# A new order for the attention units, a shorter first slot table, and list positions cast by threes

## The chip, the core and the metric

The kernel runs on one core of a Trainium2 chip. TensorE is written PE here (its weight loads PEld), VectorE DVE, ScalarE ACT, GpSimd POOL and SyncE SP; each runs its own instructions in the order in which they were issued, and waits on semaphores for the others. The metric is the device time of one execution in microseconds (us).

## The reference

Packed attention, and behind it a mixture of experts with one expert per row. There are 8 batches of 8 heads, 576 positions and 64 elements per head; p has 32 packed queries per head.

```python
def sm_attn(qq, kk, vv):                       # softmax(qq kk^T / 8) vv
    ...
p_packed = sm_attn(p, k, v)                    # 32 rows per head
out = sm_attn(q, p_packed, p_packed)           # 576 rows per head
x = out.transpose(0, 2, 1, 3).reshape(4608, 512)

logits = x @ w_gate + modality_bias[modality_id]     # [4608, 8]
e_idx = np.argmax(logits, axis=1)
gate_w = softmax(logits)[arange, e_idx]
for e in range(8):                                    # F = 1024
    out[mask_e] = gate_w[mask_e] * (np.maximum(x[mask_e] @ w1[e], 0) @ w2[e])
```

## The kernel before, in words

**Attention** is cut into 8 units: a unit is one pair of batches and one half of the heads. A unit consists of named steps, each a generator's next stretch:

- `dk`, `dq`, `dv`: loads of k, q and v, issued by SP. k and q go to the tiles rek and req, of which there are two each.
- `k0`-`k4`, `q0`-`q4`: PE turns k and q (L231), ACT copies the result out of PSUM to kT (L234).
- `c0`, `c1`: scores of the packed queries (L246 on PE), the maximum on DVE (nb, L257), exp on ACT (L261). `r`: reciprocals of the sums on DVE (L267 to L269).
- `a0`-`a2`: PE turns these weights (L275), ACT copies them (L278). `p`, given three times or more: weights times v on PE (L289, called the pack below), DVE scales and masks them (bd, L297; pd, L301).
- `t`: PE turns pd (L308), ACT copies it (ppT, L312). `g`: the gate's product (L322, L325).
- `s0`, `s1`, each given several times: scores of all queries against the packed keys (L246 on PE), then on DVE a transposing read (st, L333), maximum (L336), subtraction (L338), sum (L343), reciprocal (L347), product (L349) and a transposition back (a2T, L355); exp is ACT's (L340).
- `x0`-`x2`: the output of the unit and its gate logits (L371 on PE), copied by ACT (xs, L382), the logits by DVE (lt, L384). `w`: SP writes xs to DRAM as x_scr (L396, L397).

PSUM has four buffers for transpositions (ps1) and two for scores, packs and outputs (ps2), so a step that needs a buffer waits for the reader of the one before it.

**The order** of all this on PE, DVE, ACT and SP is written out by hand: the string `ORDER` is run once for every n from -6 on, and `>` or `<` in front of a name takes the step of unit n+1 or n-1 instead of n. `e` runs a piece of other work (the preparation of p, L169 to L174, and the routing of rows that are complete), `f` a piece of `scatter`, which writes row numbers to lists in DRAM by POOL: a list position is cast to an integer on DVE (L485) and used by one indirect DMA (L486). Units 0 to 6 run in this loop wholly; of unit 7 only `d k c q a r p` do.

**Behind the loop** comes the mixture. Rows of one expert fill slots of two tiles of 128 rows. A slot table (`table_phase`) says which expert and which list rows each slot has; there are three, a, b and c, each made from the rows that are routed by then. Table a is computed on DVE near the end of the loop. The first expert's w1 is loaded early, or loaded again if table a names another one (the `If` at L867, which waits in SP's queue behind what stands there). ACT rounds w1 to its high part (w1h, L672), DVE takes the rest (w1l, L673), rows are fetched by POOL (L677, L679), turned by PE (L692), and multiplied: L712 is the first product (h), L747 the second. The rest of unit 7 (`t g s0 s1 x0 x1 x2 w`) runs within slot 0.

Of the kernel before, what the change touches and what calls it, by code (L numbers as in the profile page):

```python
# [8 lines left out]
F32 = mybir.dt.float32  # L9
F32R = mybir.dt.float32r  # L10
BF16 = mybir.dt.bfloat16
I32 = mybir.dt.int32
AF = mybir.ActivationFunctionType
ALU = mybir.AluOpType
# [9 lines left out]
def packed_attn_moe_kernel(  # L24
# [14 lines left out]
    nc = tc.nc  # L39
# [3 lines left out]
    E, _, F = w1.shape  # L43
    P = 128
# [146 lines left out]
    def attention(i, g, lt, A, Z):  # L191
# [217 lines left out]
        for nm, f, args in (("k", trans, [("k", *z) for z in fw]), ("q", trans, [("q", *z) for z in fw]),  # L409
# [3 lines left out]
            for n, z in enumerate(args or [()]):  # L413
# [1 line left out]
        return steps  # L415


    ORDER = ("<f >>c0 e >>>k4 >t >>>k2 s0 >q4 >t >>>k4 >>>k3 e >>dv >q0 >>>k0 >>c0 s0 e >q0 f s0 >>>k2 >>r s0 >s1 >s0 "
# [3 lines left out]

    def run_all(u, order):
        for z in order.split():
# [56 lines left out]

    def scatter(i):
        for c in range(NC):
            dsi = sm.tile([P, 1], I32, name=f"dsi{c}", bufs=2)
            nc.vector.tensor_copy(out=dsi, in_=dests[i][:, c:c + 1])  # L485
            ins = ins_of(nc.gpsimd.indirect_dma_start(  # L486
                out=lst, out_offset=bass.IndirectOffsetOnAxis(ap=dsi, axis=0),
                in_=meta[:, i * NC + c, :], in_offset=None))
            tc.declare_no_dep(ins, group="scat", reason="every row of the list is written once")
            tc.add_to_no_dep_group("scat", ins)  # L490
            if i >= NA[0]:
                tc.add_to_no_dep_group("late", ins)
            if i >= NA[1]:
                tc.add_to_no_dep_group("last", ins)
            scattered[i].append(ins)
            yield ins
# [4 lines left out]
    def st_(nm, w=E, dt=F32):  # L501
        return sm.tile([P, w], dt, name=nm, bufs=2)
# [91 lines left out]
    def table_phase(nm, e_first, n, used, n_slots):  # L594
# [10 lines left out]
        def row_e(starts):  # L605
            r = st_("row_e")
            tsc(out=r, in0=starts, scalar1=sidx, scalar2=-float(P2), op0=ALU.subtract, op1=ALU.mult)
            if used is not None:
# [7 lines left out]
        starts, ends, sel = table(rotated(e_first), tl, row_e, tb)  # L616
        z = slice(0, 1)
        tt(out=tb[z, 3:4], in0=tb[z, 1:2], in1=e_first[z], op=ALU.not_equal)

        pr = st_("pref", 1)  # L620
        tt(out=pr[z], in0=tb[z, 1:2], in1=tb[z, 2:3], op=ALU.subtract)
        nc.vector.scalar_tensor_tensor(out=pr[z], in0=pr[z], scalar=tb[z, 3:4], in1=tb[z, 2:3],
                                       op0=ALU.mult, op1=ALU.add)
        pre_i = const.tile([P, 1], I32, name="pre_" + nm)
        nc.vector.tensor_copy(out=pre_i[z], in_=pr[z])
        used2 = le = None
        if n_slots:
            used2 = const.tile([P, E], F32, name="used_" + nm)
            tsc(out=used2, in0=starts, scalar1=-1.0, scalar2=float(n_slots), op0=ALU.mult, op1=ALU.add)
            tt(out=used2, in0=used2, in1=tl, op=ALU.min)  # L630
            tsc(out=used2, in0=used2, scalar1=0.0, scalar2=None, op0=ALU.max)
            if used is not None:
                tt(out=used2, in0=used2, in1=used, op=ALU.add)
            le = const.tile([P, 1], F32, name="last_" + nm)
            expert_at(starts, ends, float(n_slots - 1), le)
        else:

            one = st_("one")
            nc.vector.scalar_tensor_tensor(out=one, in0=tl, scalar=-float(P2), in1=rem, op0=ALU.mult, op1=ALU.add)
            tsc(out=one, in0=one, scalar1=-float(P), scalar2=None, op0=ALU.is_le)  # L640
            tt(out=one, in0=one, in1=sel, op=ALU.mult)
            tsc(out=ends, in0=ends, scalar1=-1.0, scalar2=sidx, op0=ALU.add, op1=ALU.is_equal)
            tt(out=tb[:, 6:7], in0=dot_e(one, ends), in1=tb[:, 4:5], op=ALU.subtract)
            tsc(out=tb[:, 6:7], in0=tb[:, 6:7], scalar1=-1.0, scalar2=None, op0=ALU.mult)
        return dict(tab=to_int(tb, "tab_" + nm), pre=pre_i, used=used2, last=le)

    def val(tb, s, col, engines, lo, hi):
        return nc.values_load(tb[s:s + 1, col:col + 1], engines=engines, min_val=lo, max_val=hi,  # L648
# [263 lines left out]
    with ExitStack() as actx:  # L912
# [3 lines left out]
        ZL["st"] = (lp, zq)  # L916
        u = us[NU + 1]

        def table_b():
            for _ in routing(NA[1] - 1, lts[NA[1] - 1], ZL["ps1"]):  # L920
                pass
            T.append(table_phase("b", T[0]["last"], NA[1], T[0]["used"], SA[1] - SA[0]))
            todo.append(scatter(NA[1] - 1))

        def behind_both(ins):
            es = ExitStack()
            for z in ins:
# [14 lines left out]
        for n in range(1, 4):  # L942
            ev = st_1(W, todo[0], 3, (2 * n,))
            if n == 1:
                with behind_both(ev):
                    split_w(W, 1, None, (0, 1))
                T.append(table_phase("b", T[0]["last"], NA[1], T[0]["used"], SA[1] - SA[0]))
                tab = next(z for z in reversed(nc.cur_bb.bb.instructions) if z.engine == ET.DVE)
            if n == 2:
                with behind_both(ev):  # L950
                    split_w(W, 1, None, (2, 3))
# [5 lines left out]
        run_all(u, "s1 x0 x1 x2 w")  # L957
        for _ in routing(NA[1], lts[NA[1]], ZL["ps1"]):
            pass
    T.append(table_phase("c", T[1]["last"], NP, T[1]["used"], None))  # L960
    todo.append(scatter(NA[1]))

# [52 lines left out]
```

## Time and profile before

| | before |
|---|---|
| median of 3 runs | 609.91 us (609.74 to 610.02) |
| the profiled execution's own time | 610.75 us |
| its span, first to last instruction | 609.2 us |
| mean granted TensorE clock | 0.984 |
| instructions | 12555 |
| PE busy in the span | 570.3 us (94%) |
| DVE, ACT, POOL busy in the span | 251.7, 220.3, 147.4 us |

The profile is of one execution: its own time lies 1.55 us above its span and 0.84 us above the median of the runs. A busy share over the whole span mixes two stages, the attention (to about 140 us) and the mixture, which have different limits.

### The profile page before, as it was taken

How to read it: one execution, taken by the hardware profiler on the slowest of the kernel's cores; microseconds unless marked ns; L12 is line 12 of the kernel's file. 1: busy time of each engine (PE TensorE's matmuls, PEld its weight loads, DVE VectorE, ACT ScalarE, POOL GpSimd, SP SyncE). 2: the span in 40 equal slices, each digit the busy share in tenths (PEclk: the TensorE clock that was granted, in tenths of full speed). 3: DMA queues.
4: the chain of work that ended last, by engine and by line, in shares of the span. 5: the costliest groups of instructions: out<-in, count | busy, mean ns of one | idle time of the engine just before them, and what ended most of it. 6: DMA issues, size and time to landing. Idle time of an engine off the chain costs nothing. (4 is left out here: it accounts for less than half of the span.)

```text
span 609.2 us, 12555 instructions
## 1 busy us (share of the span) xinstructions
PE 570.3 (94%) x4820; PEld 495.7 (81%) x4820; DVE 251.7 (41%) x657; ACT 220.3 (36%) x401; POOL 147.4 (24%) x183
## 2 busy tenths in 40 slices
PE   4989899879999999999999999999999999999982
PEld 3667576567888988988979988988989989989982
DVE  1588989986956212162112182202112112112281
ACT  3667677664422212172112271212212122112361
POOL 2200041340751422322132122212212211211221
PEclk9989999997999999999999999999999999999998
DMA  9998799858668110139521146101101111111112
GB/s 309 327 332 245 245 374 358 253 158 281 236 233 249 57 53 20 37 108 387 198 68 57 36 134 248 57 36 53 54 36 36 61 46 37 54 35 54 42 49 59
DMA packets 45458, 86.97 MB, mean 143 GB/s; under 512 B 8632, under 2 KB 18552, under 8 KB 45368
## 3 DMA queue, kind: packets, MB, share of 16 engines
q1 hardware_dynamic: 35784, 63.53, 31.1%
q0 software_dynamic: 8528, 22.16, 11.6%
q8 instruction: 49, 0.80, 0.5%
q14 instruction: 41, 0.34, 0.2%
q10 hardware_dynamic: 1056, 0.15, 0.1%
HBM read 66.25 MB, written 19.56 MB: 141 GB/s over the span
## 5 line engine op out<-in xcount | busy, mean ns | idle before, releaser
L712 PE MATMUL ps_h<-x_hl,w1h 128*128 128x256 f32 x1088 | 199.0, 285 | 0.8 <-ACTq L909 0.8
L712 PEld LDWEIGHTS ps_h<-x_hl,w1h 128*128 128x128 f32 x1088 | 171.6, 192 | 4.3 <-ACT x_hl L694 1.0
L712 PE MATMUL ps_h<-x_hl,w1l 128*128 128x256 f32 x544 | 154.4, 284 | 0.0
L717 DVE SCALAR_TENSOR_TENSOR hl<-ps_h,hh 128x512 fp32r<-128x512 f32 x68 | 46.9, 690 | 245.9 <-ACT hh L716 245.8
L747 PE MATMUL ps_o<-w2h,hh 128*128 128x512 f32 x296 | 117.9, 398 | 3.3 <-ACT ot L751 2.2
L747 PE MATMUL ps_o<-w2h,hl 128*128 128x512 f32 x296 | 116.4, 393 | 0.0
L747 PE MATMUL ps_o<-w2l,hh 128*128 128x512 f32 x296 | 115.8, 391 | 0.3 <-DVEq L862 0.3
L712 PEld LDWEIGHTS ps_h<-x_hl,w1l 128*128 128x128 f32 x544 | 104.6, 192 | 0.0
L716 ACT ACTIVATE hh<-ps_h 128x512 fp32r<-128x512 f32 x68 | 40.6, 598 | 151.6 <-PE ps_h L712 150.1
L752 POOL DMA_INDIRECT out_dram<-ot,mt x37 | 40.5, 1094 | 181.4 <-ACT ot L751 112.6
L751 ACT ACTIVATE ot<-ps_o,mt 128x512 f32<-128x512 f32 x37 | 25.4, 687 | 149.7 <-PE ps_o L747 117.7
L747 PEld LDWEIGHTS ps_o<-w2h,hh 128*128 128x128 f32 x296 | 55.7, 188 | 14.8 <-ACT ot L751 3.5
L486 POOL DMA_INDIRECT lst<-meta,dsi x36 | 37.3, 1035 | 118.5 <-DVE dsi L485 64.1
L747 PEld LDWEIGHTS ps_o<-w2h,hl 128*128 128x128 f32 x296 | 55.6, 188 | 11.4
L747 PEld LDWEIGHTS ps_o<-w2l,hh 128*128 128x128 f32 x296 | 55.7, 188 | 10.9 <-DVEq L862 0.6
L679 POOL DMA_INDIRECT xt<-x_scr,mt x46 | 44.9, 976 | 76.4 <-PE ps_t L692 26.6
L234 ACT COPY kT<-ps 128x512 f32<-128x512 f32 (+1 forms) x80 | 41.9, 549 | 23.2 <-PE ps L231 21.9
L695 DVE TENSOR_TENSOR x_hl<-ps_t,x_hl 128x512 fp32r<-128x512 f32 x42 | 27.5, 684 | 19.5 <-ACTq L862 12.0
L371 PE MATMUL ps<-bd,a2T 64*128 64x136 f32 (+1 forms) x320 | 25.5, 306 | 5.4 <-DVE a2T L355 2.4
L677 POOL DMA_DIRECT2D mt<-lst x23 | 17.3, 753 | 54.5 <-DMA out_dram<-ot,mt 37.9
L231 PE MATMUL ps<-ident,rek 128*128 128x128 f32 x144 | 21.8, 288 | 7.7 <-DMA rek<-in_k_dram 7.1
L371 PEld LDWEIGHTS ps<-bd,a2T 64*128 64x128 f32 (+1 forms) x320 | 19.3, 182 | 11.0 <-issue 5.4
(187 smaller groups left out, 639.5 us busy)
## 6 DMA issues: line engine op xcount, KB each, us to landing
raw<-in_moe_w_dram SPq DMA_DIRECT2D x24, 1024.0 KB
rek<-in_k_dram SPq DMA_DIRECT2D x16, 576.0 KB
req<-in_q_dram SPq DMA_DIRECT2D x16, 576.0 KB
x_scr<-xs SPq DMA_DIRECT2D x28, 256.0 KB
ld_v<-in_v_dram SPq DMA_DIRECT2D x8, 576.0 KB
ld_v<-in_v_dram SPq DMA_DIRECT2D x8, 288.0 KB
ld_v<-in_v_dram SPq DMA_DIRECT2D x16, 144.0 KB
x_scr<-ld_v SPq DMA_DIRECT2D x4, 256.0 KB
```

Source lines behind the costliest of these rows:

```text
L231: nc.tensor.transpose(out=t[:, c * P:c * P + P], in_=src[:, (f0 + c) * P:(f0 + c) * P + P], identity=ident)
L234: nc.scalar.copy(out=T_[:, f0:f0 + w, :], in_=t[:, :w * P].rearrange("p (f r) -> p f r", f=w))
L371: nc.tensor.matmul(xp[rows, pr, z * XW:z * XW + XW], a2T[rs, t0:t0 + n], D_["bd"][rs, u ^ pr, :], start=True, stop=True)
L486: ins = ins_of(nc.gpsimd.indirect_dma_start(out=lst, out_offset=bass.IndirectOffsetOnAxis(ap=dsi, axis=0), in_=meta[:, i * NC + c, :], in_ ...
L679: ins.append(nc.gpsimd.indirect_dma_start(out=xt[:, t], out_offset=None, in_=x_scr[0:NA[ph] * 2 * S] if ph < 2 else x_scr, in_offset=bass. ...
L695: iv = tt(out=M["xl"][:, :, ts], in0=ps, in1=M["xh"][:, :, ts].bitcast(F32), op=ALU.subtract)
L712: nc.tensor.matmul(ps[:, f], M[a][:, j, (f0 + f) * P:(f0 + f) * P + P], M[b][:, j], start=(n == 0), stop=(n == 3 * KD - 1))
L716: ia = nc.scalar.activation(out=M["hh"][:, fs], in_=ps, func=AF.Relu)
L717: iv = nc.vector.scalar_tensor_tensor(out=M["hl"][:, fs], in0=ps, scalar=0.0, in1=M["hh"][:, fs].bitcast(F32), op0=ALU.max, op1=ALU.subtract)
L747: nc.tensor.matmul(op, M[a][:, j, t * P:t * P + P], M[b][:, j, :], start=(n == 0), stop=(n == 3 * KF - 1))
L751: nc.scalar.activation(out=ot, in_=op, func=AF.Copy, scale=mt.bitcast(F32)[:, t, 2:3])
L752: nc.gpsimd.indirect_dma_start(out=out, out_offset=bass.IndirectOffsetOnAxis(ap=mt[:, t, 1:2], axis=0), in_=ot, in_offset=None, bounds_che ...
```

## The change

Three edits. `ORDER` is another string: the same steps in another sequence. `table_phase` makes the choice of the first expert to load (`pre`) for the tables b and c alone, and puts two results, `used` and `last`, which only the next table reads, into a function that is called ahead of that next table. `scatter` casts three list positions with one instruction, every third time, and the three DMAs read a column each; twelve casts are left of 36. An unused function goes as well.

```diff
-    ORDER = ("<f >>c0 e >>>k4 >t >>>k2 s0 >q4 >t >>>k4 >>>k3 e >>dv >q0 >>>k0 >>c0 s0 e >q0 f s0 >>>k2 >>r s0 >s1 >s0 "
...
+    ORDER = (">>a0 >s0 x0 f >s0 x0 x2 >>>k3 >s1 >s0 x1 f x1 >>q1 >s1 x2 >s1 >>>k3 >>q4 >>q4 >s0 >>>dv x2 >>>k2 >>p >>p "
...
     def scatter(i):
         for c in range(NC):
-            dsi = sm.tile([P, 1], I32, name=f"dsi{c}", bufs=2)
-            nc.vector.tensor_copy(out=dsi, in_=dests[i][:, c:c + 1])
+            if c % 3 == 0:
+                dsi = sm.tile([P, 3], I32, name=f"dsi{c}", bufs=2)
+                nc.vector.tensor_copy(out=dsi, in_=dests[i][:, c:c + 3])
             ins = ins_of(nc.gpsimd.indirect_dma_start(
-                out=lst, out_offset=bass.IndirectOffsetOnAxis(ap=dsi, axis=0),
+                out=lst, out_offset=bass.IndirectOffsetOnAxis(ap=dsi[:, c % 3:c % 3 + 1], axis=0),
                 in_=meta[:, i * NC + c, :], in_offset=None))
...
-        pr = st_("pref", 1)
-        tt(out=pr[z], in0=tb[z, 1:2], in1=tb[z, 2:3], op=ALU.subtract)
...
-        nc.vector.tensor_copy(out=pre_i[z], in_=pr[z])
-        used2 = le = None
-        if n_slots:
-            used2 = const.tile([P, E], F32, name="used_" + nm)
...
-            expert_at(starts, ends, float(n_slots - 1), le)
-        else:
+        d = {}
+        if n != NA[0]:
+
+            pr = st_("pref", 1)
...
+            d["pre"] = pre_i
+        if not n_slots:
...
+        def behind():
+            if n_slots:
+                used2 = d["used"] = const.tile([P, E], F32, name="used_" + nm)
...
+                expert_at(starts, ends, float(n_slots - 1), le)
...
+                T[0]["behind"]()
                 T.append(table_phase("b", T[0]["last"], NA[1], T[0]["used"], SA[1] - SA[0]))
...
+    T[1]["behind"]()
     T.append(table_phase("c", T[1]["last"], NP, T[1]["used"], None))
```

What it moves, at four places. In the rows a name's number tells tiles apart, `ps2_1491<-kT_1382,ppT_1456` reads "written tile from read tiles", and x4 counts instructions in a run.

First PE in the middle of the loop, the scores of a unit and the outputs of the unit before it (`s0 s1` and `x0`). Before:

```order
L246 MATMUL ps2_1491<-kT_1382,ppT_1456 32x320 x4
L246 MATMUL ps2_1491<-kT_1382,ppT_1456 32x256 x4
L246 MATMUL ps2_1500<-kT_1382,ppT_1456 32x320 x4
L246 MATMUL ps2_1500<-kT_1382,ppT_1456 32x256 x4
L322 MATMUL ps1_1510<-wgs_102,ppT_1163 32x8 x8
L275 MATMUL ps1_1520<-ident_65,a1_1400 128x128 x3
L231 MATMUL ps1_1542<-ident_65,rek_1261 128x128 x4
L371 MATMUL ps2_1547<-bd_1124,a2T_1415 128x136 x6
```

And of the change:

```order
L246 MATMUL ps2_1488<-kT_1244,ppT_1475 32x320 x4
L246 MATMUL ps2_1488<-kT_1244,ppT_1475 32x256 x4
L246 MATMUL ps2_1499<-kT_1244,ppT_1475 32x320 x4
L246 MATMUL ps2_1499<-kT_1244,ppT_1475 32x256 x4
L322 MATMUL ps1_1510<-wgs_102,ppT_1475 32x8 x8
L275 MATMUL ps1_1520<-ident_65,a1_1466 128x128 x3
L275 MATMUL ps1_1531<-ident_65,a1_1466 128x128 x3
L275 MATMUL ps1_1540<-ident_65,a1_1466 128x128 x3
L371 MATMUL ps2_1544<-bd_1123,a2T_1413 128x136 x6
```

All three turnings of the first softmax's weights (L275) now stand together ahead of the outputs, and the transposition of k that stood there is elsewhere.

Second, PE where the scores of the packed queries (L246 that reads pT) stand. Before, straight behind the outputs, each half by itself:

```order
L371 MATMUL ps2_1305<-bd_853,a2T_1121 128x136 x6
L275 MATMUL ps1_1312<-ident_65,a1_1097 128x128 x3
L246 MATMUL ps2_1322<-kT_1165,pT_113 32x320 x4
L246 MATMUL ps2_1322<-kT_1165,pT_113 32x256 x4
L231 MATMUL ps1_1342<-ident_65,req_988 128x128 x4
```

Of the change, with the pack and three groups of transpositions ahead of them, and both halves together:

```order
L289 MATMUL ps2_1354<-ld_v_1037,a1T_1273 64x128 x36
L231 MATMUL ps1_1393<-ident_65,rek_883 128x128 x2
L231 MATMUL ps1_1398<-ident_65,req_959 128x128 x4
L231 MATMUL ps1_1403<-ident_65,req_959 128x128 x4
L246 MATMUL ps2_1428<-kT_1198,pT_113 32x320 x4
L246 MATMUL ps2_1428<-kT_1198,pT_113 32x256 x4
L246 MATMUL ps2_1437<-kT_1198,pT_113 32x320 x4
L246 MATMUL ps2_1437<-kT_1198,pT_113 32x256 x4
```

The kT tile that the scores read is copied by ACT; between its last transposition and the scores there is now a pack and more.

Third, PE at the start, where the pack of unit 0 and the preparation of p (L171) meet. Before:

```order
L289 MATMUL ps2_314<-ld_v_235,a1T_259 64x128 x12
L171 MATMUL ps1_329<-ident_65,raw1_114 128x128 x4
L289 MATMUL ps2_314<-ld_v_235,a1T_259 64x128 x12
L171 MATMUL ps1_352<-ident_65,raw1_114 128x128 x4
L289 MATMUL ps2_314<-ld_v_235,a1T_259 64x128 x12
```

Of the change:

```order
L289 MATMUL ps2_297<-ld_v_178,a1T_264 64x128 x36
L171 MATMUL ps1_334<-ident_65,raw1_114 128x128 x4
L231 MATMUL ps1_342<-ident_65,rek_152 128x128 x2
L231 MATMUL ps1_345<-ident_65,req_169 128x128 x4
L171 MATMUL ps1_350<-ident_65,raw1_114 128x128 x4
L231 MATMUL ps1_357<-ident_65,req_169 128x128 x4
L171 MATMUL ps1_363<-ident_65,raw1_114 128x128 x4
```

The three preparations now stand behind the whole pack. On DVE the reading of the third one stands ahead of unit 0's bd in the change, as the second does before.

Fourth, PE at the end of the loop, from the last output of unit 6 to the first product of the mixture. Before:

```order
L371 MATMUL ps2_2241<-bd_1980,a2T_2189 128x136 x6
L692 MATMUL ps_t0_2403<-ident_65,xt0_2273 128x128 x4
L308 MATMUL ps1_2427<-ident_65,pd_2198 128x128 x2
L322 MATMUL ps1_2432<-wgs_102,ppT_2430 32x8
L692 MATMUL ps_t0_2403<-ident_65,xt0_2273 128x128 x4
L322 MATMUL ps1_2432<-wgs_102,ppT_2430 32x8 x7
L246 MATMUL ps2_2442<-kT_2159,ppT_2430 32x320 x4
L246 MATMUL ps2_2442<-kT_2159,ppT_2430 32x256 x4
L712 MATMUL ps_h0_2404<-x_hl_2275,w1h_115 128x256 x2
```

Of the change, whose lines are numbered nine higher there (L701 is the L692 of before, L721 its L712):

```order
L371 MATMUL ps2_2217<-bd_1963,a2T_2178 128x136 x6
L308 MATMUL ps1_2386<-ident_65,pd_2191 128x128 x2
L322 MATMUL ps1_2391<-wgs_102,ppT_2389 32x8 x8
L246 MATMUL ps2_2401<-kT_2040,ppT_2389 32x320 x4
L246 MATMUL ps2_2401<-kT_2040,ppT_2389 32x256 x4
L701 MATMUL ps_t0_2362<-ident_65,xt0_2249 128x128 x8
L721 MATMUL ps_h0_2363<-x_hl_2251,w1h_115 128x256 x2
```

The fetched rows are now turned behind unit 7's own steps. In both kernels the w1 split stands ahead of unit 6's lt on DVE.

The results that `behind` was to put off stand among the loop's rows on DVE in the changed kernel too; these are five of them, with rows of other work between:

```order
L645 TENSOR_SCALAR used_a_2508<-starts_2277 128x8
L646 TENSOR_TENSOR used_a_2508<-used_a_2508,tl_o_2260 128x8
L647 TENSOR_SCALAR used_a_2508<-used_a_2508 128x8
L549 TENSOR_SCALAR sel_g_2513<-ends_2278 128x8
L570 TENSOR_REDUCE last_a_2512<-ex_m_2517 128x1
```

The scheduler has pulled them forward to where their inputs are ready. Only the three operations of `pre` are gone from the loop.

## Rows read from the trace of the kernel before

**Rows 1.** By stretch: start:end, length, busy PE PEld DVE ACT POOL, clock, DMA, GB/s.
```profile
42.00:56.50 14.50, 14.24 (x247) 10.74 (x249) 12.22 (x29) 11.45 (x25) 0.00 (x0) 1.00 0.76 230
...
134.40:146.20 11.80, 10.61 (x92) 7.54 (x93) 5.30 (x10) 7.76 (x11) 0.94 (x1) 0.57 0.95 326
146.20:200.00 53.80, 52.99 (x374) 46.38 (x374) 40.48 (x181) 16.39 (x27) 21.75 (x21) 1.00 0.70 229
200.00:609.20 409.20, 392.82 (x2555) 356.92 (x2553) 101.17 (x144) 108.17 (x178) 94.72 (x97) 0.99 0.24 78
```

**Rows 2.** DVE in order of time: the first st of units 0 to 6.
```profile
28.72 1.43 DVE L333 STREAM_TRANSPOSE st<-ps 128x576 f32<-128x576 f32 x2
...
42.95 1.41 DVE L333 STREAM_TRANSPOSE st<-ps 128x576 f32<-128x576 f32 x2
...
57.47 1.40 DVE L333 STREAM_TRANSPOSE st<-ps 128x576 f32<-128x576 f32 x2
...
75.38 0.74 DVE L333 STREAM_TRANSPOSE st<-ps 128x576 f32<-128x576 f32 x1
...
90.15 1.44 DVE L333 STREAM_TRANSPOSE st<-ps 128x576 f32<-128x576 f32 x2
...
106.97 0.74 DVE L333 STREAM_TRANSPOSE st<-ps 128x576 f32<-128x576 f32 x1
...
122.60 1.43 DVE L333 STREAM_TRANSPOSE st<-ps 128x576 f32<-128x576 f32 x2
```

**Rows 3.** PE in order of time, in unit 0 and in unit 1.
```profile
32.82 0.73 PE L246 MATMUL ps<-kT,pT 64*32 64x320 f32 x14 [1.55 <-ACT kT L234]
33.48 2.80 PE L231 MATMUL ps<-ident,req 128*128 128x128 f32 x12
36.22 2.53 PE L289 MATMUL ps<-ld_v,a1T 64*64 64x128 f32 x72
...
47.97 0.72 PE L246 MATMUL ps<-kT,pT 64*32 64x320 f32 x2
48.95 0.73 PE L246 MATMUL ps<-kT,pT 64*32 64x320 f32 x14 [0.26 <-ACT kT L234]
49.62 1.53 PE L231 MATMUL ps<-ident,req 128*128 128x128 f32 x12
51.08 2.20 PE L289 MATMUL ps<-ld_v,a1T 64*64 64x128 f32 x72
```

**Rows 4.** DVE in unit 1: its waits, in brackets with what ended them.
```profile
46.02 0.21 DVE L384 COPY lt<-ps 128x48 f32<-128x48 f32 x1 [0.24 <-ACT xs L382]
...
47.29 0.21 DVE L384 COPY lt<-ps 128x48 f32<-128x48 f32 x1 [0.41 <-ACT xs L382]
...
49.81 0.76 DVE L257 TENSOR_REDUCE nb<-ps 128x1 f32<-128x576 f32 x1 [0.78 <-PE ps L246]
...
53.34 0.42 DVE L297 TENSOR_TENSOR bd<-ps,rm 128x256 f32<-128x256 f32 x1 [0.46 <-PE ps L289]
```

**Rows 5.** PE at the start: one preparation of p.
```profile
21.40 0.63 PE L171 MATMUL ps<-ident,raw 128*128 128x128 f32 x4 [0.49 <-DVE raw L169]
```

**Rows 6.** DVE in order of time: a cast and what follows it.
```profile
78.27 0.15 DVE L485 CAST dsi<-dsf 128x1 int32<-128x1 f32 x1
78.33 0.20 DVE L384 COPY lt<-ps 128x48 f32<-128x48 f32 x1
```

**Rows 7.** All engines in order of time, end of the loop.
```profile
126.95 1.28 SPq L396 DMA_DIRECT2D x_scr<-xs  x2
...
134.89 1.04 ACT L672 CAST w1h<-raw 128x1024 fp32r<-128x1024 f32 x1 [2.42 <-SPq L867]
135.97 1.23 DVE L673 TENSOR_TENSOR w1l<-raw,w1h 128x1024 fp32r<-128x1024 f32 x1 [1.73 <-ACT w1h L672]
137.37 1.73 PE L371 MATMUL ps<-bd,a2T 64*128 64x136 f32 x12 [0.64 <-DVE lt L384]
...
144.06 0.79 PE L712 MATMUL ps_h<-x_hl,w1h 128*128 128x256 f32 x2
```

More of the change, by code (lines that the diff above doesn't have):

```diff
@@ L618, in table_phase @@
         tt(out=tb[z, 3:4], in0=tb[z, 1:2], in1=e_first[z], op=ALU.not_equal)
-        pr = st_("pref", 1)
-        tt(out=pr[z], in0=tb[z, 1:2], in1=tb[z, 2:3], op=ALU.subtract)
-        nc.vector.scalar_tensor_tensor(out=pr[z], in0=pr[z], scalar=tb[z, 3:4], in1=tb[z, 2:3],
-                                       op0=ALU.mult, op1=ALU.add)
-        pre_i = const.tile([P, 1], I32, name="pre_" + nm)
-        nc.vector.tensor_copy(out=pre_i[z], in_=pr[z])
-        used2 = le = None
-        if n_slots:
-            used2 = const.tile([P, E], F32, name="used_" + nm)
[L629 to L634, printed above, removed]
-            expert_at(starts, ends, float(n_slots - 1), le)
-        else:
+        d = {}
+        if n != NA[0]:
+            pr = st_("pref", 1)
+            tt(out=pr[z], in0=tb[z, 1:2], in1=tb[z, 2:3], op=ALU.subtract)
+            nc.vector.scalar_tensor_tensor(out=pr[z], in0=pr[z], scalar=tb[z, 3:4], in1=tb[z, 2:3],
+                                           op0=ALU.mult, op1=ALU.add)
+            pre_i = const.tile([P, 1], I32, name="pre_" + nm)
+            nc.vector.tensor_copy(out=pre_i[z], in_=pr[z])
+            d["pre"] = pre_i
+        if not n_slots:
             one = st_("one")
@@ L644, in table_phase @@
             tsc(out=tb[:, 6:7], in0=tb[:, 6:7], scalar1=-1.0, scalar2=None, op0=ALU.mult)
-        return dict(tab=to_int(tb, "tab_" + nm), pre=pre_i, used=used2, last=le)
+        d["tab"] = to_int(tb, "tab_" + nm)
+        def behind():
+            if n_slots:
+                used2 = d["used"] = const.tile([P, E], F32, name="used_" + nm)
+                tsc(out=used2, in0=starts, scalar1=-1.0, scalar2=float(n_slots), op0=ALU.mult, op1=ALU.add)
+                tt(out=used2, in0=used2, in1=tl, op=ALU.min)
+                tsc(out=used2, in0=used2, scalar1=0.0, scalar2=None, op0=ALU.max)
+                if used is not None:
+                    tt(out=used2, in0=used2, in1=used, op=ALU.add)
+                le = d["last"] = const.tile([P, 1], F32, name="last_" + nm)
+                expert_at(starts, ends, float(n_slots - 1), le)
+        d["behind"] = behind
+        return d
     def val(tb, s, col, engines, lo, hi):
@@ L917, in packed_attn_moe_kernel @@
         u = us[NU + 1]
[L919 to L923, printed above, removed]
         def behind_both(ins):
```

6 rows, old and new, of the table ORDER are left out of this document.

## The prediction

> **What bounds the kernel now.** I read busy time by stretch first, since the span mixes two stages. From 200 us on PE works 392.82 of 409.2 us, and from 146.2 to 200 us 52.99 of 53.8 [rows 1]: the mixture is bound by PE, its order is not touched, and the 24 casts that vanish there and in the loop lie on DVE, which works 101.17 of those 409.2. So I carry everything behind the first L712, at 144.06 [rows 7], over unchanged; what the change is worth must arise before it.
>
> The loop is read with DVE in order of time: the first st of each unit marks a cycle. From 28.72 to 122.60 [rows 2] the six cycles take 14.23, 14.52, 17.91, 14.77, 16.82 and 15.63 us, together 93.88. The reader is to ask of each which engine it waits for. The second cycle shows it best. DVE works 12.22 of 14.50 us there [rows 1], and waits .24, .41, .78 and .46 us [rows 4]: twice for ACT's xs, once for scores, once for the pack. PE is nearly closed but has one hole: the scores of the next unit start at 47.97, do two matmuls, and the other fourteen start at 48.95 [rows 3], when ACT has copied the last kT. Two of sixteen matmuls at .73 us would take .09, so .9 us are lost, and 14.52 - .9 = 13.6 us is what PE has to do in a cycle. DVE needs 12.2 and a few waits. So plain cycles are PE's, and cycles with routing or tables in them (third, fifth, sixth) are DVE's.
>
> **The order, in the loop.** The scores move behind the pack and three groups of transpositions, so kT has been copied for over 2.2 us (one pack [rows 3]) when they start. The hole of PE goes. What is late next is PE's own work.
>
> - First cycle: PE's hole is 1.55 us here [rows 3], and behind it the clock was low: twelve transpositions took 2.80 where a cycle later they took 1.53, and a pack 2.53 for 2.20 [rows 3], 1.6 us together. Without both, 14.23 - 1.55 - 1.6 = 11.1; DVE holds it at about 12.0 (its 12.2 less one logit copy, .2). Gain 2.2.
> - Second: 13.6 plus .25 for one remaining wait of the size of [rows 4]'s .24, 13.85. Gain .7. Fourth likewise, from 14.77 to 13.8: gain 1.0.
> - Third and fifth: 17.91 and 16.82 are DVE's 12.2 and the routing's operations, with the two waits for xs, .65 together [rows 4], in them. These stay: the second xs stands behind an exp on ACT in the new order too. Gain 0.
> - Sixth: as before, less casts and the three operations below. Gain .5.
>
> Together 4.4. From both sides: the DVE cycles gain nothing and the PE ones only their holes (.9 each and 1.55), 3.3; or all waits of [rows 4], 1.89, go in the second and fourth, which the 13.6 of PE's work forbids beyond .9 each.
>
> **The order, at the start.** Before, the bd of unit 0 had two preparations of p ahead of it, each .63 us and .49 us of waiting [rows 5]: 2.24 us. In the change it has three, with ten transpositions between that fill the waits: 3 x .63 + 10 x .13 (twelve take 1.53 [rows 3]) = 3.2. So unit 0's scores, and st with them, come .9 us later. The bounds are 0 (if DMA, which feeds these tiles, is what is late) and 1.3 (if one wait of .49 stays).
>
> **The end of the loop.** Here the new order loses. What holds PE before the last output of unit 6 at 137.37 is a chain that the change keeps: SP issues unit 5's rows to DRAM from 126.95 on, then reaches the branch at L867; ACT's w1h, at 134.89, waits 2.42 us for it, DVE's w1l at 135.97 waits for w1h, and lt stands behind w1l [rows 7]. From unit 6's st, 122.60 [rows 2], to 137.37 are 14.77 us, and I keep them. Behind it, before, the fetched rows are turned first and unit 7's scores fill the time in which their parts are split; in the change pd, gate and scores stand ahead of them. That is one transposition pair, a gate and half of a unit's scores more on the path to L712 (144.06, 6.69 us behind the last output). The clock from 134.4 to 146.2 is .57 [rows 1], near the lower of the two levels, 1.2 GHz, after PE had waited. With those steps at the lower level my count is up to 2.8 us, with them filling waits that are there now, 0. I take 1.6, nearer the first, since the rows' turning and splitting are a chain through PE, ACT and DVE that used to begin straight behind the output.
>
> The Trainium skill speaks against this place too: "TensorE: Matmul & The Clock Gate", section "What's actually happening", has the slow clock as the state that TensorE falls back to when it isn't kept at work. The .57 behind a wait agrees. The new order makes the outputs x0 and x1 of unit 6 early but not x2, so PE's wait there grows; if by that the slow stretch began 1 us earlier, another .5 us would go.
>
> **Casts and table.** Of the 24 casts that vanish, 12 lie in the loop. One lasts .15 us, but what follows it starts .06 after it [rows 6], and I take the start-to-start time: 12 x .06 = .7, of which only those in DVE's cycles count; two thirds of the scatter's pieces do, but some of these stand in waits, and I count .2 in the sixth cycle and nothing elsewhere. Bounds: 0 and 12 x .15 = 1.8. The Trainium skill, "VectorE: DVE Perf Modes", section "The DRAIN you can't avoid", would have the next operation wait until the pipe is empty, which makes it 1.8; the trace doesn't agree, since the copy behind the cast starts .09 us before the cast's end.
>
> Putting `used` and `last` behind does next to nothing: their rows still stand in the loop on DVE. Of `pre` three single-element operations go; nothing of theirs is in view, so between 0 and three casts' .15: .3, which I put in the sixth cycle (this is its .5 with the casts). The DMAs of the lists leave POOL in threes; the span behind 200 us uses POOL 94.72 of 409.2 [rows 1], so nothing queues there. On SP the rows' writes now stand behind the next unit's v; they are read at the fetch, which the end of the loop already waits for by the chain above.
>
> **Sum.** -4.4 + .9 + 1.6 = -1.9 us. On the profiled execution's own time, 610.75, that gives 608.85; the median of the runs is .84 below that one, so 608.0.
>
> **Rivals.** A change of .2%, 1.2 us, is about what a measurement of this kernel can tell from none.
>
> - *The end keeps its clock.* If unit 7's scores fill the time and L712 comes no later, the 1.6 falls away: 606.4. If PE also stays at the upper level of 2.4 GHz, its 10.61 us of work at .57 [rows 1] would be 6.0, and as its inputs set about half of the pace there, some 2 us more go: 604.4. For it: these are real fillers. Against it: the chain of SP, ACT and DVE is the same. 12%.
> - *Nothing measurable.* The plain cycles turn out DVE's too: 12.2, .65 for xs and .46 for the pack [rows 4] are 13.3, so one wait of .7 more makes 14.0 and halves the gain of the second and the fourth. If these two gain .5 each and the first only its hole, 1.55, the loop gives 2.55, and .9 + 1.6 take it back: 609.9. With the band around it, 24%.
> - *Slower.* In the new order the output x0 waits on PE behind both scores, the gate and three turnings, where one turning stood before. ACT's xs and DVE's lt follow it, and lt stands in DVE's row ahead of the next maximum, so DVE's whole row waits. PE's rows then set when lt comes, and if lt waits 1.2 us in each of six cycles for today's .24 [rows 4], that is 5.8 us, and the sum is +3.9: 613.8. It decides from .3 us per cycle on (1.9 / 6). For it: lt waits for xs today [rows 4]. Against: in DVE's cycles PE is ahead. 21%.
> - *The edit that doesn't do what it says*: the deferred table results. Priced above at nothing; were they deferred truly, DVE's sixth cycle would lose some 1 us more. It is in the second case's band, with no chance of its own.
>
> **How the numbers follow.** The forecast, -1.2 to -4.0 us, .43; the end at its better, .12; nothing measurable .24; slower .21. So faster .55, same .24, slower .21. The forecast alone is 605.9 to 608.7; with the cases of either side 604.2 to 612.0, which leaves out the far end of the slower case and of the faster one.
>
> **What would show it.** In the changed profile: the first st of unit 0 at 29.6, that of unit 6 near 119.1, the cycles 12.0, 13.85, 17.9, 13.8, 16.8, 15.1; no wait of the scores for kT; no half clock before 40 us. The first L721 then stands 21.4 to 24.2 us behind unit 6's st (21.46 before), and the rest of the span takes 465 us as now. It is wrong if lt's waits for xs exceed 1 us in the loop, if the start loses more than 1.3, or if the mixture moves by more than .5 us.

## The result, and the profile after

The change makes the kernel slower: 615.62 us median of 4 runs (615.35 to 617.03) against 609.96 (609.74 to 610.17), a ratio of 1.0095 (95% interval 1.0081 to 1.0108), 5.7 us. The profiled execution took 615.59 us, its span is 613.9 for 609.2, so 4.7 us of the loss can be looked for in the trace.

The page's first part, as before: busy time, share, instructions of each engine.

```profile
PE 567.6 (92%) x4820; PEld 495.5 (81%) x4820; DVE 250.6 (41%) x630; ACT 218.6 (36%) x401; POOL 146.4 (24%) x183
```

PE does no more than before; it stands idle 7.4 us longer (613.9 - 567.6 = 46.3 for 38.9). DVE in order of time, the first st of units 0 to 6, answers to [rows 2]:

```profile
29.96 1.44 DVE L333 STREAM_TRANSPOSE st<-ps 128x576 f32<-128x576 f32 x2
...
42.22 1.44 DVE L333 STREAM_TRANSPOSE st<-ps 128x576 f32<-128x576 f32 x2
...
55.80 1.44 DVE L333 STREAM_TRANSPOSE st<-ps 128x576 f32<-128x576 f32 x2
...
74.37 1.44 DVE L333 STREAM_TRANSPOSE st<-ps 128x576 f32<-128x576 f32 x2
...
89.39 1.44 DVE L333 STREAM_TRANSPOSE st<-ps 128x576 f32<-128x576 f32 x2
...
107.42 1.43 DVE L333 STREAM_TRANSPOSE st<-ps 128x576 f32<-128x576 f32 x2
...
122.05 1.44 DVE L333 STREAM_TRANSPOSE st<-ps 128x576 f32<-128x576 f32 x2
```

With the first product of the mixture, which now starts at 147.31 (L721) for 144.06, the 4.7 us are laid out stretch by stretch:

| stretch | before | after | difference | forecast |
|---|---|---|---|---|
| start to st of unit 0 | 28.72 | 29.96 | +1.24 | +.9 |
| first cycle | 14.23 | 12.26 | -1.97 | -2.2 |
| second | 14.52 | 13.58 | -.94 | -.7 |
| third | 17.91 | 18.57 | +.66 | 0 |
| fourth | 14.77 | 15.02 | +.25 | -1.0 |
| fifth | 16.82 | 18.03 | +1.21 | 0 |
| sixth | 15.63 | 14.63 | -1.00 | -.5 |
| st of unit 6 to first product | 21.46 | 25.26 | +3.80 | +1.6 |
| first product to the end | 465.14 | 466.59 | +1.45 | 0 |

The loop gains 2.9 us in its first two cycles and keeps 1.8 of them. The larger losses are at the end of the loop and behind it. The end of the loop is the surest row of the table: the stretch from st of unit 6 to the first product takes 21.28 to 21.65 us in all six traces of the old order on this sort of chip (the kernel before and runs 2, 4, 13, 14 and 15 below), and 25.26 and 25.55 in the changed kernel and run 1. There all engines in order of time, answering to [rows 7]:

```profile
135.37 1.04 ACT L681 CAST w1h<-raw 128x1024 fp32r<-128x1024 f32 x1 [4.68 <-SPq L876]
136.44 1.22 DVE L682 TENSOR_TENSOR w1l<-raw,w1h 128x1024 fp32r<-128x1024 f32 x1 [3.03 <-ACT w1h L681]
137.84 1.45 PE L371 MATMUL ps<-bd,a2T 64*128 64x136 f32 x12 [3.81 <-DVE lt L384]
140.42 0.69 PE L308 MATMUL ps<-ident,pd 128*128 128x128 f32 x2 [1.13 <-DVE lt L384]
...
143.01 1.11 PE L701 MATMUL ps_t<-ident,xt 128*128 128x128 f32 x4
145.53 1.11 PE L701 MATMUL ps_t<-ident,xt 128*128 128x128 f32 x4 [1.40 <-DVE x_hl L704]
147.31 1.30 PE L721 MATMUL ps_h<-x_hl,w1h 128*128 128x256 f32 x2 [0.67 <-ACT x_hl L703]
```

What the reader is to see: ACT waits 4.68 us for SP's branch, DVE 3.03 for ACT, PE 3.81 for DVE's lt, one behind the other; the outputs that PE had ready before are done early and nothing takes their place. Then unit 7's pd, gate and scores stand ahead of the rows (143.01), and the first product comes 9.47 us behind the last output, for 6.69.

The granted clock by stretch (start:end, length, busy time of PE, PEld, DVE, ACT, POOL, granted clock, DMA share, GB/s):

```profile
10.00:15.00 5.00, 4.02 (x42) 2.57 (x43) 2.21 (x4) 1.18 (x3) 0.00 (x0) 0.69 1.13 342
75.00:80.00 5.00, 4.80 (x44) 3.92 (x45) 4.38 (x11) 2.85 (x4) 3.06 (x4) 0.67 0.92 357
...
137.00:147.30 10.30, 5.81 (x54) 3.26 (x54) 1.90 (x6) 3.36 (x8) 0.00 (x0) 0.56 0.79 266
147.30:152.00 4.70, 4.54 (x20) 4.25 (x21) 4.70 (x7) 2.80 (x3) 0.00 (x0) 0.52 0.00 0
```

Before, the stretches from 10 to 15 and from 75 to 80 us were at 1.00. Now PE is at 1.2 GHz for some three of the five microseconds in both (12 to 15 and 77 to 80 us), and from 138 us past the first product until 152 us (before, from 136 to 146). The slow stretch that the kernel before had in its first cycle, around 35 us, is gone. The row from 147.30 on is most of the 1.45 us behind the first product: the first six groups of three matmuls end at 151.83, 4.52 us for the 6 x .36 that they take at full clock, 2.36 lost; before, three groups were slow, to 146.14, and lost 1.0. The difference is 1.36.

### The profile page after: what moved, and what is told of

The parts are those of the page before. It is cut to its first block, busy times and chain, and to the rows that moved or that the text cites. A ratio compares the mean times of both kernels' runs of the same rounds, so it can differ in the third digit from the quotient of the medians.

```text
span 613.9 us, 12517 instructions
## 1 busy us (share of the span) xinstructions
PE 567.6 (92%) x4820; PEld 495.5 (81%) x4820; DVE 250.6 (41%) x630; ACT 218.6 (36%) x401; POOL 146.4 (24%) x183
## 5 line engine op out<-in xcount | busy, mean ns | idle before, releaser
L721 PE MATMUL ps_h<-x_hl,w1h 128*128 128x256 f32 x1088 | 200.0, 285 | 1.5 <-ACTq L918 0.7
L721 PEld LDWEIGHTS ps_h<-x_hl,w1h 128*128 128x128 f32 x1088 | 172.2, 193 | 4.8 <-ACT x_hl L703 1.1
L721 PE MATMUL ps_h<-x_hl,w1l 128*128 128x256 f32 x544 | 154.7, 284 | 0.0
L721 PEld LDWEIGHTS ps_h<-x_hl,w1l 128*128 128x128 f32 x544 | 105.0, 193 | 0.0
L487 POOL DMA_INDIRECT lst<-meta,dsi x36 | 36.0, 1001 | 114.6 <-DVE key L531 35.1
L234 ACT COPY kT<-ps 128x512 f32<-128x512 f32 (+1 forms) x80 | 39.0, 555 | 12.8 <-PE ps L231 12.2
L231 PE MATMUL ps<-ident,rek 128*128 128x128 f32 x144 | 24.0, 304 | 5.7 <-DMA rek<-in_k_dram 5.3
```

Of the source, the lines that this page charges most:

```text
L231: nc.tensor.transpose(out=t[:, c * P:c * P + P], in_=src[:, (f0 + c) * P:(f0 + c) * P + P], identity=ident)
L234: nc.scalar.copy(out=T_[:, f0:f0 + w, :], in_=t[:, :w * P].rearrange("p (f r) -> p f r", f=w))
L487: ins = ins_of(nc.gpsimd.indirect_dma_start(out=lst, out_offset=bass.IndirectOffsetOnAxis(ap=dsi[:, c % 3:c % 3 + 1], axis=0), in_=meta[:, ...
L721: nc.tensor.matmul(ps[:, f], M[a][:, j, (f0 + f) * P:(f0 + f) * P + P], M[b][:, j], start=(n == 0), stop=(n == 3 * KD - 1))
```

## The experiments

Each was timed beside the kernel before on the same chip. There the kernel before took 610.6 and 610.2 us on two chips and 619.4 and 618.5 on two others, whose loop shows longer cycles; so ratios are compared, and profiles only with those of the same sort of chip.

**1. The order alone.** The kernel before, with the new `ORDER` string and nothing else.

```diff
-    ORDER = ("<f >>c0 e >>>k4 >t ...
+    ORDER = (">>a0 >s0 x0 f >s0 x0 ...
```

Expected: 

> The kernel before with nothing but the new order string; casts one at a time, first slot table whole. Theory A (the order is the whole loss, and the casts and the table are worth nothing that can be measured): 615 to 616.5 us, st of unit 0 near 30.0 us, st of unit 6 near 122, first product of the mixture near 147. Theory B (the scatters that now leave in threes, and the table's operations that the scheduler pulls forward on DVE, carry a part of the loss, above all in the fifth cycle, which took 18.03 us for 16.82): 611 to 614 us, with the third and fifth cycle back at 17.9 and 16.8.

Measured: 616.12 us, ratio 1.0105 (1.0083 to 1.0127), as much as the whole change; st of unit 6 at 122.03, first product at 147.58. Theory A holds for the order. The run also shows what a slow stretch costs: its fourth cycle took 13.72 us, not 15.02, and its sixth 16.50, not 14.63, for here the slow clock came later:

```profile
75.00:80.00 5.00, 4.68 (x68) 3.86 (x70) 4.37 (x14) 3.75 (x6) 2.49 (x3) 1.00 0.99 398
105.00:110.00 5.00, 3.51 (x34) 2.58 (x36) 5.00 (x29) 1.95 (x3) 2.34 (x2) 0.73 1.03 369
110.00:115.00 5.00, 5.00 (x56) 4.42 (x56) 4.88 (x25) 3.51 (x7) 1.90 (x2) 0.59 0.69 170
```

So the fourth cycle at full clock is what was forecast (13.8), and a slow stretch takes 1.3 us of it. PE had waited as long ahead of that cycle as in the changed kernel (2.58 us for 2.53), and the clock stayed at 1.00 all the same:

```profile
74.61 2.02 PE L371 MATMUL ps<-bd,a2T 64*128 64x136 f32 x28 [2.58 <-DVE st L333]
```

**2. Casts and table alone.** The changed kernel with the old string.

```diff
-    ORDER = (">>a0 >s0 x0 f >s0 x0 ...
+    ORDER = ("<f >>c0 e >>>k4 >t ...
```

Expected: 

> The changed kernel with the old order string: casts by threes and the shorter first table alone. Theory A: 609.3 to 610.3 us, no change that can be told from none, cycles as before. Theory B: 611 to 613 us, with the third, fifth or sixth cycle longer than before.

Measured: 613.16 us, 1.0046 (1.0029 to 1.0062), slower, though st of unit 6 stood at 122.50 and the first product at 143.78, .28 earlier than before. The loss lay behind it: 2.0 us at about 308 us, where PE paused 1.13 and .60 us at a branch and then had a stretch at .73. Neither theory had foreseen that; runs 13 to 15 take it up.

**3. The logits ahead of the w1 split.** In the changed kernel:

```diff
...
-        split_w(W, 0, None, (0,))
+        with behind_both((W["lt"], W["xc"])):     # unit 6's last lt and xs
+            split_w(W, 0, None, (0,))
```

Expected: 

> The changed kernel, with the first quarter of the w1 split (ACT's w1h, DVE's w1l) held until unit 6's last xs and lt are issued, so that these no longer stand behind a cast that waits for SP's branch. Theory A (at the end of the loop PE waits because xs and lt stand behind the split; 3.81 us in the changed kernel before x2): that wait goes, x2 starts near 134.5 for 137.84, the first product of the mixture comes 1.5 to 3.3 us earlier, 612 to 614 us. Rival (the path runs through SP's queue, the branch and w1 anyway, and the first product needs w1h and w1l): the wait moves to the first product, 615 to 616 us.

Measured: 611.78 us, 1.0023 (1.0008 to 1.0038), 4.3 us less than the order alone beside it. PE in order of time at the end of the loop (st of unit 6 at 122.57):

```profile
133.45 1.58 PE L371 MATMUL ps<-bd,a2T 64*64 64x136 f32 x20 [0.62 <-DVE a2T L355]
136.18 0.44 PE L308 MATMUL ps<-ident,pd 128*128 128x128 f32 x2 [1.15 <-DVE lt L384]
...
138.01 0.66 PE L701 MATMUL ps_t<-ident,xt 128*128 128x128 f32 x4
140.07 1.11 PE L701 MATMUL ps_t<-ident,xt 128*128 128x128 f32 x4 [1.40 <-DVE x_hl L704]
141.86 1.30 PE L721 MATMUL ps_h<-x_hl,w1h 128*128 128x256 f32 x2 [0.68 <-ACT x_hl L703]
```

The wait of 3.81 is gone, the last output follows the one before it, and the first product comes 19.29 us behind the st, for 25.26. Theory A holds, and by more than it said; the rival, that w1 itself sets the end, falls.

**4. The same edit on the kernel before.**

Expected: 

> The same edit on the kernel before. Theory A: x2 of unit 6 starts near 135.5 for 137.37, and the first product comes 1 to 2 us earlier: 608 to 609 us. Rival: 609.5 to 610.3 us, since w1h and w1l are then late for the first product.

Measured: 613.02 us, 1.0039 (1.0024 to 1.0055); the first product 21.49 us behind the st, for 21.46. A miss for both theories: the wait of .64 on lt was no limit there, since rows and unit 7's scores filled it, and the mixture's beginning then took 2.9 us longer (ACT copies its third output 50.68 us behind the first product for 47.83). Of these, 1.9 us are the clock: it stayed at .50 to 150 us, for 146, and the first eight groups of three matmuls took 5.77 us for the 2.88 that they take at full clock, 2.9 lost for the 1.0 of the kernel before. Another 1.01 us is a wait of PE for ACT's hh at 180 us. Neither theory had a slow clock in its account.

**5. PE kept busy.** In the changed kernel, turnings of the identity that nobody reads, 16 ahead of x0 of units 2 and 4, 28 ahead of x2 of unit 6; nothing of the computation is left out.

```diff
+        def fill(n):
+            f = ZL["ps1"].tile([P, 512], F32, name="ps1")
+            for z in range(n):
+                nc.tensor.transpose(out=f[:, z % 4 * P:z % 4 * P + P], in_=ident, identity=ident)
...
```

Expected: 

> The changed kernel with turnings of the identity that nobody reads put on PE where it waits: 16 ahead of the first output of units 2 and 4 (waits of 2.53 and 2.04 us), 28 ahead of the last output of unit 6 (3.81 us). Theory C (a part of the loss is the clock: PE's longer waits in the new order are followed by 1.2 GHz, from 75 to 80 us and from 136 to 152 us): the granted clock stays at 1.00 there, the fourth cycle falls from 15.0 to 13.7 us, the stretch from the last output to the first product from 9.5 to 6 to 7.5 us, and the time to 610.5 to 613. Rival (the slow stretches hide in waits that are there anyway, or come whatever PE does): 615 to 617 us.

Measured: 625.70 us on a chip where the kernel before took 619.39, 1.0113 (1.0089 to 1.0136). The clock stayed at 1.00 from 75 to 85 us, but the fourth cycle took 18.15 us there, and 17.88 in run 8 beside it, which had no fillers and .69 from 75 to 80: the cycle was set by other waits there (PE stood 1.10 us within the pack and 1.93 for ppT), not by the clock. At the end the slow clock came behind the next pause instead, and the first product stood 27.17 us behind the st. Theory C's clock is as it said, its gain is not there.

**6. The preparations of p an iteration later.**

```diff
-        more = {-1: rest()}
+        more = {0: rest()}
```

Expected: 

> The changed kernel with the preparations of p for units 2 to 7 one iteration later, so that none stands ahead of unit 0's bd. If the start is late by the preparations (predicted .9 us, measured 1.24): the first st of unit 0 near 28.8 us for 29.96, and 614 to 615.3 us. Rival (the start is late by the transfers or by the slow clock from 10 to 15 us): st of unit 0 stays between 29.4 and 30.3 us, and the time within .6 us of the changed kernel's.

Measured: 631.67 us, 1.0215 (1.0186 to 1.0243), worse than anything. The first st came at 27.62 us, 2.6 us ahead of run 8 on the same chip (30.19), so they do make the start late; but then unit 1's bd waits for them, and the first cycle takes 18.17 us for 12.43.

**7. The rows turned ahead of unit 7's steps.** In the changed kernel, with the split where it was:

```diff
...
-        run_all(u, "t g")
-        next(u["s0"])
+        with behind_both((W["px"],)):             # the last turning of the fetched rows
+            run_all(u, "t g")
+            next(u["s0"])
```

Expected: 

> The changed kernel with both turnings of the fetched rows on PE ahead of unit 7's pd, gate and scores, which go behind; the w1 split stays where it is, ahead of xs and lt. If the predicted step (1.6 us for unit 7's steps ahead of the rows) is right: the first product comes 1 to 2.8 us earlier against st of unit 6 (25.26 us in the changed kernel), 613 to 614.5 us. Rival (the chain from the last output through xs, lt and the split sets it): less than .5 us.

Measured: 623.69 us, 1.0077 (1.0051 to 1.0104). The first product stood 23.02 us behind the st; in the changed kernel 25.26, and 24.3 to 27.9 in the other runs here that leave the end as it is. That supports the step, 1 to 3 us, no closer: the end of that very stretch moves by itself by that much on this sort of chip.

**8. Both edits at the end.**

Expected: 

> The changed kernel with both edits at the end: xs and lt of unit 6 ahead of the w1 split, and the rows turned ahead of unit 7's steps. The split behind the logits alone gave 611.8 and put the first product 19.29 us behind st of unit 6. If the turning then follows the last output directly: 17 to 18.5 us, 610 to 611.5 us. Rival (the turning waits for the fetched rows or for ACT's and DVE's splits): 19 to 20 us, 611.5 to 612.5 us.

Measured: 621.48 us, 1.0024 (1.0002 to 1.0046), the same as run 3 alone; first product 20.60 us behind the st. Rows first adds nothing once the logits go ahead: PE then waits 3.12 us between the two turnings for DVE's and ACT's splitting. The rival holds, with a stretch .6 us longer than it said.

**9 to 12. The changed kernel again, and three mends beside it on one chip.** Run 9 is the measure. Run 10 has the fillers of run 5 in the loop alone. Run 11 puts the preparations back among the pack's thirds. Run 12 has run 3's edit and both of these.

```diff
+                        if m == 0 and nm == "p" and W.setdefault("np", 0) < 3:
+                            W["np"] += 1
+                            next(more[-1])
                         next(us[m][nm])
```

Expected of 9: 

> The changed kernel itself, unaltered, as the measure for the three beside it on the same chip. All theories: 1.008 to 1.011 times the kernel before.

Expected of 10: 

> The changed kernel with 16 turnings of the identity that nobody reads ahead of the first output of units 2 and 4 alone (PE waits of 2.53 and 2.04 us). Theory C (the slow clock from 75 to 80 us, behind PE's wait, costs the fourth cycle its gain): no stretch under 1.00 there, the fourth cycle 13.7 us for 15.0, 1.0 to 1.6 us less than the changed kernel beside it. Rival: less than .5 us less, since the transfers or DVE set that cycle.

Expected of 11: 

> The changed kernel with the three preparations of p one ahead of each third of unit 0's pack, instead of behind the whole pack. If unit 0's bd is late by them: the first st of unit 0 1 to 1.5 us earlier than in the changed kernel beside it, and .8 to 1.5 us less in all. Rival (a kernel with these preparations an iteration later had its first st some 3 us earlier and lost 5.7 us in the next cycle): what the start gains is lost by unit 1, less than .5 us in all.

Expected of 12: 

> The changed kernel with three mends at once: xs and lt of unit 6 ahead of the w1 split, the fillers ahead of the outputs of units 2 and 4, the preparations within the pack. If each removes a cost of its own: 5.5 to 7 us less than the changed kernel beside it, .2 to 1.2 us less than the kernel before. Rival (the mends share a cost, the slow clock moves on to the next wait): 3.8 to 4.5 us less, as with the logits alone, still slower than before.

Measured: run 9 625.64 us, 1.0121 (1.0093 to 1.0149), a little above what was expected. Run 10 627.24, 1.0141 (1.0114 to 1.0167), no gain: from 75 to 85 us its clock was 1.00, where run 9's was .75 and .91, the fourth cycle 17.75 for 17.93, and the slow stretch came from 90 to 100 us instead. Run 11 626.02, 1.0124 (1.0096 to 1.0153): the first st came 1.34 us earlier (29.10 for 30.44), and the first cycle gave .85 back (13.09 for 12.24), so by its rival. Run 12 621.28, 1.0037 (1.002 to 1.0054), 4.4 us less than run 9: what run 3's edit gives by itself. None beats the kernel before.

**13 to 15. Which of the small edits costs.** The kernel before with the casts alone, with the table alone, and with both again. The casts:

```diff
...
-            nc.vector.tensor_copy(out=dsi, in_=dests[i][:, c:c + 1])
+                nc.vector.tensor_copy(out=dsi, in_=dests[i][:, c:c + 3])
...
```

Expected of 13: 

> The kernel before with the casts by threes alone. The casts and the table together, in the old order, were 1.0046 times the kernel before, though unit 6's st and the first product came no later (122.50 and 143.78 us for 122.60 and 144.06) and 2.0 us were lost at one place, a stretch at 1.2 GHz from 305 to 312 us behind a pause of PE. Theory D (it is the casts: scatters that leave POOL and its queue otherwise): 1.003 to 1.006. Theory E (it is chance of that chip, a slow stretch that came in most of its executions): .998 to 1.002.

Expected of 14: 

> The kernel before with the shorter first table alone (three operations of the loop gone, two results later in the program). Theory F (it is the table: code behind the loop lies otherwise, so that PE's pauses at branches change): 1.003 to 1.006. Theory E: .998 to 1.002.

Expected of 15: 

> Both, in the old order, once more. Theories D and F: 1.003 to 1.006 again, with a slow stretch near 310 us. Theory E: within .998 and 1.002, or no slow stretch there.

Measured: 612.16 us, 1.0036 (1.0023 to 1.0049) for the casts; 610.86, 1.001 (.9998 to 1.0022) for the table; 613.12, 1.0051 (1.0037 to 1.0064) for both. By the times Theory D holds: it is the casts. The slow stretch near 310 us that was expected of run 15 is not in its trace, which is of its fastest execution (611.41). PE paused there as in run 2, but the clock stayed at 1.00. Run 2, and then run 15:

```profile
307.78 0.50 PE L756 MATMUL ps_o<-w2h,hh 128*128 128x512 f32 x1 [1.13 <-ACTq L871]
308.88 0.50 PE L756 MATMUL ps_o<-w2l,hh 128*128 128x512 f32 x1 [0.60 <-DVEq L871]
```

```profile
307.87 0.50 PE L756 MATMUL ps_o<-w2h,hh 128*128 128x512 f32 x1 [1.13 <-ACTq L871]
308.96 0.49 PE L756 MATMUL ps_o<-w2l,hh 128*128 128x512 f32 x1 [0.59 <-DVEq L871]
```

By what path the casts cost time is not shown. The casts' run has one suspect, POOL's fetch of the next slots behind the last of nine scatters. In the casts' run, and then in the kernel before:

```profile
170.43 0.75 POOL L678 DMA_DIRECT2D mt<-lst  x1 [3.51 <-DMA lst<-meta,dsi]
```

```profile
167.05 0.75 POOL L677 DMA_DIRECT2D mt<-lst  x1 [1.42 <-DMA lst<-meta,dsi]
```

The fetch waits 3.51 us for the lists to land, for 1.42; PE then waits .81 us for the rows, which it didn't before. But run 2, with the same casts, waited 1.42 us, and run 1, which casts each position by itself, 3.49 (run 4, which does too, 3.66). Run 2, and then run 1:

```profile
167.12 0.75 POOL L686 DMA_DIRECT2D mt<-lst  x1 [1.42 <-DMA lst<-meta,dsi]
```

```profile
176.89 0.75 POOL L677 DMA_DIRECT2D mt<-lst  x1 [3.49 <-DMA lst<-meta,dsi]
```

So the late landing comes with either form of cast and does not explain their price. In the changed kernel the fetch starts 1.46 us behind the last scatter. The second pause at 308 us doesn't explain it either: in the old order it is .57 to .60 us with the casts and .25 or .26 without, but in the new order .25 with them (the changed kernel) and .57 without (run 1). The casts' run, whose trace is of its slowest execution (613.64), also took 15.40 us for 14.52 in its second cycle.

## Why the prediction was wrong

The forecast was -1.9 us; the span moved by +4.7. By its own steps:

- **What bounds the loop, and the second cycle: right.** The scores no longer wait for kT, and the second cycle is 13.58 us where 13.85 was forecast. It is 13.58 or 13.59 in ten of the eleven traces of the new order, and 14.52 to 15.40 in the six of the old one.
- **The first cycle: 12.26 us for a forecast of 12.0, but in good part by luck.** The forecast gave the order both the hole of 1.55 us and the 1.6 us at the lower clock behind it. In runs 2, 14 and 15 the old order has the hole and keeps the clock, and its first cycle takes 12.62 to 12.64 us. In run 14:

```profile
34.01 0.73 PE L246 MATMUL ps<-kT,pT 64*32 64x320 f32 x14 [1.46 <-ACT kT L234]
34.67 1.53 PE L231 MATMUL ps<-ident,req 128*128 128x128 f32 x12
```

  So about 1.6 of the gain of 1.97 us came with the clock, which the old order has at times too, and some .4 with the order; the hole itself cost little here.
- **The start: right in kind, .34 too small, and not clear of chance.** Unit 0's bd comes behind the third preparation, and st 1.24 us later, within the bounds. The forecast gave each of the two preparations before .49 us of waiting, but the second waited .26, so its 2.24 us are 2.0, and 3.2 less 2.0 is 1.2:

```profile
23.11 0.63 PE L171 MATMUL ps<-ident,raw 128*128 128x128 f32 x4 [0.26 <-DVE raw L169]
```

  Run 6 shows that the preparations hold the start, run 11 that the start's loss is mostly handed to the next cycle if mended. But st of unit 0 stood at 29.64 to 29.90 us in runs 2, 14 and 15 as well, in the old order, so the 1.24 us of one pair of traces is no measure of the step. And "no half clock before 40 us" did not come true: the clock was .69 from 10 to 15 us.
- **The third cycle, "Gain 0": .66 longer. The fifth and sixth, forecast .5 shorter: .21 longer.** They come with the order: the third takes 18.56 to 18.63 us in all eleven traces of the new order and 17.89 to 17.91 in the six of the old one, the fifth 18.01 or more for 16.82 or less. In the third cycle DVE was busy 16.56 us, as before within .1, but waited .88 us for ACT's exp of the routing (below), which stands behind a unit's exp in the new order. In the fifth and sixth the table's operations moved from the sixth into the fifth (DVE busy 17.15 us for 15.97, then 14.31 for 15.43); together the two cycles are 32.66 us for 32.45.

```profile
60.10 0.21 DVE L384 COPY lt<-ps 128x48 f32<-128x48 f32 x1 [0.56 <-ACT xs L382]
...
70.65 0.23 DVE L474 TENSOR_REDUCE gs<-lg 128x9 f32<-128x72 f32 x1 [0.88 <-ACT lg L471]
```

- **The fourth cycle: 13.8 forecast, 15.02 measured, by the clock on this sort of chip.** The step took PE's work at full speed. In the third cycle PE comes early to x0, and waits for DVE to free the scores' buffers; behind that wait outputs and turnings took 4.07 and 1.10 us, for 3.07 and .66 in the cycle before:

```profile
56.83 3.07 PE L371 MATMUL ps<-bd,a2T 64*128 64x136 f32 x40
59.84 0.66 PE L231 MATMUL ps<-ident,rek 128*128 128x128 f32 x4
...
75.20 4.07 PE L371 MATMUL ps<-bd,a2T 64*128 64x136 f32 x40 [2.53 <-DVE st L333]
79.20 1.10 PE L231 MATMUL ps<-ident,rek 128*128 128x128 f32 x4
```

  Run 1 had 13.72 at full clock; on the slower chips full clock did not shorten the cycle (runs 5 and 10). The Trainium skill, "TensorE: Matmul & The Clock Gate", section "What's actually happening", has an idle TensorE fall back to the slow state; the .67 behind a wait of 2.53 us agrees, and I had applied it to the end of the loop only. Run 1's 1.00 behind 2.58 us shows that such a wait need not bring it.

- **The end of the loop: the step that failed by most.** "I keep them", of the 14.77 us from unit 6's st to its last output: 15.79 measured. And of unit 7's steps, "I take 1.6" between 0 and 2.8: 2.78, the upper bound, since PE was at the lower clock there throughout. Run 3 shows what of it the order made worse: with xs and lt ahead of the split, the stretch is 19.29 us, less than before's 21.46. The coupling through SP's branch was there before (run 4: it cost nothing); the new order put unit 6's first two outputs early and so left the wait with nothing to fill it.
- **"I carry everything behind the first L712 over unchanged": wrong, +1.45.** The slow stretch runs 4.5 us into it, which is 1.36 of them. In the other five traces of the old order, each with an edit of its own, this part took 465.59 to 467.95 us for 465.14, so it is not as steady as the step had it.
- **Casts and table.** The table at next to nothing was right (run 14). In the sixth cycle both did in the old order what the step said, .2 us each for .2 and .3 (15.42 us in run 13 and 15.44 in run 14, for 15.63). But the casts cost .36% there in all, by a path that the prediction did not have and no run shows; POOL's low busy share, by which it dismissed the lists' DMAs, says nothing of when the lists have landed. Under the new order the casts' cost does not show: the order alone was as slow as the whole change. The section of the Trainium skill that the prediction sets against its .06 us, "The DRAIN you can't avoid" of "VectorE: DVE Perf Modes", lets a next operation that is not held start earlier, so [rows 6] does not contradict it.

Of the rivals, *slower* had the size (613.8) and not the mechanism: lt's wait in the loop rose from .40 to .56 us at the second third and fell to nothing at the first, far from 1.2 us in each cycle. *The end keeps its clock* was the reverse of what came. The sum of the misses: .34 at the start, 2.6 in the loop, 2.2 at the end of it, 1.45 behind it, 6.6 us.

What stays open: the profiled pair differs by 4.8 us and the medians by 5.7, and which of the slow stretches come in every execution was not settled. The mend of run 3 leaves .2 to .4% over the kernel before; the third and fifth cycles and the slow stretches are what the traces show of that; no run mends them. What the casts cost the old order, and why the clock falls behind one wait and not behind an equal one, is open too.

## What to carry to other kernels

When an order makes one engine early, look for what it will then wait for: here PE's busy time fell by 2.7 us, and its idle time grew by 7.4. An instruction that waits for a branch or a queue belongs behind everything on its engine that does not need it; a coupling that costs nothing in one order (run 4) can cost 4 us in another. Before a wait is called the price of an edit, look for it in traces without the edit: the 3.5 us for the lists stood there too. And a step of 1 us wants more than one pair of traces: the first cycle of the old order alone moves by 1.6 us.

## What the runs showed of the hardware

The granted clock falls in the middle of a kernel that is otherwise busy, and the wait ahead of it does not tell whether it will. Behind a PE wait of 2.53 us at 75 us it fell (the changed kernel), behind 2.58 at the same place it stayed at 1.00 (run 1). Behind pauses of 1.13 and .60 us at 308 us it fell in run 2, and behind 1.13 and .59 it stayed in run 15. A slow stretch cost 1.3 us in the fourth cycle of the new order (15.02 us in the changed kernel, 13.72 in run 1) and 1.6 us in the first of the old one (14.23 us in the kernel before, 12.63 in run 14). With one wait filled, a slow stretch came later instead (runs 5 and 10). Executions of one kernel on one chip tend to be longer at a lower mean clock (over the 26 of the kernel before beside run 1 the correlation is -.70), but not strictly: the fastest had 607.86 us at .995, the slowest 612.02 at .985. POOL's fetch behind the nine scatters waited 1.42 us for the lists to land in some traces and 3.4 to 3.7 in others, whichever way the positions were cast (runs 2 and 13, the kernel before and run 1). And chips differed by 8 to 9 us for the kernel before; in the changed kernel the slower sort shows it in the fourth and sixth cycles (17.93 and 18.66 us in run 9, for 15.02 and 14.63).
